# The attention blocks in another order: the four first blocks of the batches at the start

## The chip, the cores and the metric

The kernel runs on one core of a Trainium2 chip. The metric is device time in microseconds (us) of one execution, as the median of several runs. PE is TensorE, DVE is VectorE, ACT is ScalarE, POOL is GpSimd, and SP is the queue that issues nearly all transfers.

## What is computed

Attention with a local window of 96 keys and 8 global keys, with a linear distance bias per head, and behind it a feed-forward layer. Shapes: 4 batches, 8 heads, 768 positions, head width 64; the layer goes from 512 to 2048 and back, over 3072 tokens.

```
scores = scale * np.matmul(q, k.transpose(0, 1, 3, 2))
...
keep = is_global | is_local
...
bias = -slopes[:, None, None] * dist[None, :, :]
scores = scores + bias[None, :, :, :]
scores = np.where(keep, scores, -1000000000.0)
scores = scores - np.max(scores, axis=-1, keepdims=True)
a = np.exp(scores)
a = a / (np.sum(a, axis=-1, keepdims=True) + 1e-09)
return np.matmul(a, v).astype(np.float32)
...
h = x @ w_in
g = h * (1.0 / (1.0 + np.exp(-1.702 * h)))
return (g @ w_out).astype(np.float32)
```

## The kernel before

**Blocks.** A block is 128 positions of one batch, all 8 heads. There are 24, numbered n in the order in which they are worked; before, that is batch by batch, so that blocks 0, 6, 12 and 18 are the first of a batch. A first block sees 128 keys (its own). Every other block sees 256: its own 128, and 128 that stand for the block before it with the 32 leading keys of the batch written over its first 32 (which hold the global ones).

**Two forms.** Blocks 0 to 3 (n < EARLY) go through `first`. It computes the scores once with queries in rows (matmuls into the tile `s`, the mask `mm` added by one more matmul with a unit matrix, a DVE reduction into `top` for the largest), turns the largest with `aux` and `mT`, and computes the scores again with keys in rows (`sT`: product, mask, and the largest subtracted by a third matmul). ACT takes the exponential into `pt`, and f32 matmuls of `pt` with `VF` give `pv`; a 65th column of ones gives the sum. Blocks 0 and 1 (n < FIRST) do the products in f32 from `QZ` and `KF`, turned by PE; blocks 2 and 3 do them as pairs of f16 halves from `QK`, turned by a DMA transpose.

Blocks 4 to 23 go through `unit`, four units of two heads each: scores `s`, a DVE pass that adds the mask and takes the largest (`p`, `NM`), the exponential on ACT, a split in f16 halves `hl` (a cast on ACT, a subtraction on DVE), a DMA transpose into `pt`, and three 64-column matmuls into `pv` for every head and 128 keys.

**What a block needs of the one before.** `leading` writes the 32 leading keys and values of the batch, kept in `KG` and `VG`, over the first rows of a block that is done, so that the next block can use it. `handover` fills the places where this isn't there yet: for block 2 it builds keys (`QKover2`, by a load, a split, a DMA transpose and two copies) and values, for block 4 values.

**The layer.** Two blocks make a chunk c of 256 tokens (c = 0 to 11). `finish` makes `xT` of a block. Chunks 0 to 2 run `up` (tile `h`, from the up weights `w`) and `down` (tile `y`) for 8 slices s of the layer, in plain form. Chunks 3 to 11 run `up_two`, with fewer products over sums of weights (`T`, made by `twist`) and of inputs (`xS`), tiles `pa` and `pb`. The 16 weight tiles (up and down of 8 slices) are loaded as 64-bit words and converted: two passes on ACT, two on DVE, a cast on ACT, and a subtraction on DVE that ends a tile (`w`).

**What sets the order.** All of this is written as tasks with a cost for each engine and a due time. `Work.order` runs through time, gives each engine the ready task that is due first, and writes every engine's instructions in that order; each engine then works its queue in that order. In the first 50 us of that plan PE gets filler matmuls (`idle`) where it has nothing else. The due times of the layer follow T0, PACE0 and SKEW: SKEW is how many slices chunk 1 runs behind chunk 0.

PSUM is eight banks, used by rings: `r_s` and `r_pv` with one buffer each, `r_h` with two, and four `r_y`. Before, the scores of blocks 0 and 1 alternate between `r_s` and `r_y[1,1]`. `r_QK` has three buffers and `r_raw` two.

## Time and profile before

| | us |
|---|---|
| median of 3 runs | 622.38 (621.77 to 622.87) |
| the profiled execution, time | 621.17 |
| the profiled execution, span | 619.4 |
| PE busy | 599.5 (97%) |
| PE weight load busy | 453.0 (73%) |
| DVE busy | 503.8 (81%) |
| ACT busy | 480.1 (78%) |
| POOL busy | 3.9 (1%) |

The span is from the first instruction of the profiled execution to its last; the execution's own time is 1.8 us longer. Matmuls are pipelined and their ends are modelled: what one costs PE in a full stretch is the distance between the starts of two, not its own duration. DVE and ACT are busy for four fifths of the span, but not evenly.

### The profile page before, as it was taken

How to read it: one execution, taken by the hardware profiler on the slowest of the kernel's cores; microseconds unless marked ns; L12 is line 12 of the kernel's file. 1: busy time of each engine (PE TensorE's matmuls, PEld its weight loads, DVE VectorE, ACT ScalarE, POOL GpSimd, SP SyncE). 2: the span in 40 equal slices, each digit the busy share in tenths (PEclk: the TensorE clock that was granted, in tenths of full speed). 3: DMA queues.
4: the chain of work that ended last, by engine and by line, in shares of the span. 5: the costliest groups of instructions: out<-in, count | busy, mean ns of one | idle time of the engine just before them, and what ended most of it. 6: DMA issues, size and time to landing. Idle time of an engine off the chain costs nothing.

```text
span 619.4 us, 17131 instructions
## 1 busy us (share of the span) xinstructions
PE 599.5 (97%) x6871; PEld 453.0 (73%) x6874; DVE 503.8 (81%) x1175; ACT 480.1 (78%) x1100; POOL 3.9 (1%) x16
## 2 busy tenths in 40 slices
PE   7989998999999999999999999999999999999995
PEld 4867876776777776777777777776767767777895
DVE  5778899999999969869979989888878978856441
ACT  3778999967967978779978988987988977924432
POOL 2000000000000000000000000000000000000000
PEclk9999999999999999999999999999999999999998
DMA  8999887999777668799999999999999999510001
GB/s 190 246 265 302 252 283 156 186 187 175 161 155 141 123 147 158 140 177 204 173 204 205 217 206 190 202 234 195 192 229 211 207 199 216 135 35 3 35 3 39
DMA packets 260854, 108.01 MB, mean 174 GB/s; under 512 B 241664, under 2 KB 242176, under 8 KB 260768
## 3 DMA queue, kind: packets, MB, share of 16 engines
q1 hardware_dynamic: 260480, 106.85, 84.4%
q8 instruction: 55, 0.90, 0.6%
q14 instruction: 31, 0.25, 0.1%
q10 hardware_dynamic: 288, 0.00, 0.0%
HBM read 56.43 MB, written 6.29 MB: 101 GB/s over the span
## 4 chain that ended last, share of the span: by engine, by line
PE 72%; DVE 11%; DMA 8%; ACT 5%; issue 3%; SPq 0%; POOL 0%; DVEq 0%; ACTq 0%; POOLq 0%
PE y L905 31%; PE pa L839 12%; PE pb L839 9%; PE h L799 8%; PE s L526 4%; DMA pt<-hl 4%; DMA QK<-qk 1%; PE pv L557 1%; DVE w L367 1%; PE pv L559 1%; PE pv L558 1%; PE pv L633 1%; ACT p L542 1%; DMA raw<-in_k_dram 1%; DVE hl L547 1%
## 5 line engine op out<-in xcount | busy, mean ns | idle before, releaser
L905 PE MATMUL y<-w,g 128*128 128x512 f16 (+1 forms) x1248 | 268.4, 363 | 0.3 <-DVE g L811 0.2
L905 PEld LDWEIGHTS <-g 128*128 128x128 f16 x1248 | 117.6, 98 | 102.1 <-DVE g L811 1.1
L839 PEld LDWEIGHTS <-w 128*128 128x128 f16 x1728 | 101.4, 98 | 6.0
L542 ACT ACTIVATE p<-p,NM 128x256 f32<-128x256 f32 (+1 forms) x160 | 77.2, 485 | 4.5 <-DVE NM L532 4.3
L839 PEld LDWEIGHTS <-T 128*128 128x128 f16 x1296 | 76.6, 98 | 4.5 <-issue 0.2
L799 PE MATMUL h<-xT,w 128*128 128x256 f16 x576 | 69.7, 273 | 2.3 <-DVE xT L705 1.4
L547 DVE TENSOR_TENSOR hl<-p,hl 128x512 f16<-128x512 f32 (+1 forms) x80 | 51.7, 646 | 15.5 <-ACT hl L546 15.1
L799 PEld LDWEIGHTS <-w 128*128 128x128 f16 x576 | 55.4, 98 | 12.0 <-issue 2.6
L532 DVE CUSTOM_DVE_ANT_0 p<-s,mm 128x256 f32<-128x256 f32 (+1 forms) x160 | 58.2, 398 | 6.0 <-PE s L526 5.8
L871 ACT ACTIVATE t<-h 128x512 f32<-128x512 f32 (+1 forms) x72 | 36.2, 518 | 25.3 <-DVE h L847 25.0
L880 DVE SCALAR_TENSOR_TENSOR g<-t,g 128x512 f16<-128x512 f32 x72 | 49.0, 687 | 7.8 <-ACT g L879 7.2
L847 DVE TENSOR_TENSOR h<-pb,h 128x256 f32<-128x256 f32 x72 | 29.1, 419 | 28.5 <-PE pb L839 26.5
L546 ACT CAST hl<-p 128x512 f16<-128x512 f32 (+1 forms) x80 | 46.9, 586 | 6.5 <-DMA pt<-hl 4.5
L879 ACT ACTIVATE g<-t 128x512 f16<-128x512 f32 x72 | 44.8, 628 | 7.5 <-DVE t L872 7.5
L839 PE MATMUL pa<-xS,T 128*128 128x128 f16 x648 | 45.0, 219 | 0.0
L526 PEld LDWEIGHTS <-QK 128*128 128x128 f16 x592 | 36.9, 98 | 7.2 <-DVE NM L532 3.1
L872 DVE SCALAR_TENSOR_TENSOR t<-t,h 128x512 f32<-128x512 f32 (+1 forms) x72 | 38.3, 552 | 4.7 <-ACT t L871 4.0
L526 PE MATMUL s<-QK 128*128 128x128 f16 x320 | 38.5, 219 | 0.0
L839 PE MATMUL pb<-xS,w 128*128 128x128 f16 x540 | 37.5, 219 | 0.0
L839 PE MATMUL pa<-xT,w 128*128 128x128 f16 x540 | 37.2, 219 | 0.0
L526 PE MATMUL s<-QK,QK 128*128 128x128 f16 x272 | 33.9, 219 | 2.0 <-DVE NM L532 2.0
L557 PE MATMUL pv<-VR,pt 128*128 128x64 f16 x288 | 33.9, 193 | 1.8 <-DMA pt<-hl 1.5
(193 smaller groups left out, 1103.0 us busy)
## 6 DMA issues: line engine op xcount, KB each, us to landing
ws<-in_moe_w_in_dram SPq DMA_DIRECT2D x8, 1024.0 KB, 7.2
ws<-in_moe_w_out_dram SPq DMA_DIRECT2D x8, 1024.0 KB, 8.0
raw<-in_q_dram SPq DMA_DIRECT2D x24, 256.0 KB, 3.9
raw<-in_k_dram SPq DMA_DIRECT2D x24, 256.0 KB, 4.9
QK<-QK SPq DMA_DIRECT2D x44, 128.0 KB, 3.7
out_dram<-yo SPq DMA_DIRECT2D x22, 256.0 KB, 2.9
raw<-in_v_dram SPq DMA_DIRECT2D x20, 256.0 KB, 4.3
ws_00again<-in_moe_w_in_dram SPq DMA_DIRECT2D x8, 512.0 KB, 4.8
```

The costliest lines, as they stand in the source:

```text
L526: nc.tensor.matmul(sp()[:, j, s * P:(s + 1) * P], d["QK"]()[:, 0, h, :], K[:, 1 + z, h, :], start=(z == 0), stop=(z == 1), skip_group_chec ...
L532: nc.vector.tensor_tensor_reduce(out=pr()[:, j, :], in0=sp()[:, j, :], in1=m, scale=-1.0 / SC, scalar=3.0e38, op0=ALU.add, op1=ALU.min, ac ...
L542: ex.append(add({"ACT": 0.28 + 0.105 * ns}, lambda e, j=j: nc.scalar.activation(pr()[:, j, :], pr()[:, j, :], AF.Exp, bias=NM[:, n, hs[j]: ...
L546: t4 = add({"ACT": 0.1 + 0.215 * ns}, lambda e: nc.scalar.copy(hl()[:, 0], pr()), ex, [pr, hl])
L547: t5 = add({"DVE": 0.07 + 0.265 * ns}, lambda e: nc.vector.tensor_sub(hl()[:, 1], pr(), hl()[:, 0]), [t4], [pr, hl])
L557: nc.tensor.matmul(o, ph, V[:, 0, h], start=(s == 0), stop=False, skip_group_check=True)
L799: nc.tensor.matmul(ph()[:, fi, :], w1(s, cc, z, fi), X[:, y, cc, :], start=(j + cc == 0), stop=(j == 2 and cc == NCC - 1))
L839: nc.tensor.matmul(o()[:, fi], w, x()[:, y * NCC + 2 * k + cc, t], start=(first and fi + j + cc == 0), stop=(last and j + cc == 3), skip_g ...
L872: return add({"DVE": 0.08 + 0.265 * w}, lambda e: nc.vector.scalar_tensor_tensor(o(), o(), 1.0, src(), ALU.add, ALU.mult), [t1], srcs)
L879: t4 = add({"ACT": 0.53}, lambda e, g=g, tt=tt: nc.scalar.mul(g()[:, 0], tt(), SG / (SX * SW)), u, [tt, g])
L880: t5 = add({"DVE": 0.61}, lambda e, g=g, tt=tt: nc.vector.scalar_tensor_tensor(g()[:, 1], tt(), SG / (SX * SW), g()[:, 0], ALU.mult, ALU.s ...
L905: nc.tensor.matmul(y(), part(zg, f), w2(s, z, f % 2)[:, m], start=(begin and f + j == 0), stop=(end and j == 2 and f == 2 * len(steps) - 1 ...
```

## The change

The blocks get another numbering. `place(n)` gives batch and position: n = 0 to 3 are the first blocks of the four batches, and n = 4 to 23 are the positions 1 to 5 of batch 0, of batch 1, and so on. All four blocks of `first` now see 128 keys, and its code has one key block left: two passes of four heads each, where there were four of two. All 20 blocks of `unit` see 256 keys. Where a batch goes on (n = 4, 9, 14, 19), `handover` loads the k and v of its first block once more and builds `QKover`, `VRover`, `KG` and `VG` from them. The scores of all four first blocks go through `r_s`. Chunk rows of the output follow `place`. T0, PACE0 and SKEW are lower.

```diff
+    def place(n):
+
+        return (n, 0) if n < EARLY else ((n - EARLY) // (NB - 1), 1 + (n - EARLY) % (NB - 1))
+
     def load(n, raw, parts=(0, 1, 2)):
-        b, i = divmod(n, NB)
+        b, i = place(n)
...
-    def handover(n, keys, whole):
-
-        b = n // NB
-        d = prev[n] = dict(blk[n - 1], VG=[])
+    def handover(n):
+
+        b = place(n)[0]
+        d = prev[n] = {}
         raw = Buf(r_raw, [P, 3, H, D], F32, f"over{n}")
-        if keys:
-            d["G"] = []
-            d["QK"] = Buf(r_QK, [P, 3, H, P], F16, f"QKover{n}")
-            d["qk_ready"] = turn_halves(f"over{n}", raw, d["QK"], rows_before(n, k, lambda: raw()[:, 1], raw), 1)
-            keep_keys(b, d)
...
+        d["QK"] = Buf(r_QK, [P, 3, H, P], F16, f"QKover{n}")
+        d["VR"] = Buf(r_VR, [P, 2, H, D], F16, f"VRover{n}")
+        ld = load(b, raw, (1, 2))
+        d["qk_ready"] = turn_halves(f"over{n}", raw, d["QK"], ld[:1], 1)
+        d["v_ready"] = d["VG"] = halves(d["VR"], raw, ld[1:])
+        d["G"] = []
+        keep_keys(b, d)
+        keep_values(b, d)
...
     def unit(n, u, want_s, want_v):
 
-        b, i = divmod(n, NB)
-        ns = 1 if i == 0 else 2
+        ns = 2
...
     def first(n, want):
 
-        b, i = divmod(n, NB)
-        ns = 1 if i == 0 else 2
-        W = ns * P
         d = blk[n]
...
-        spare = r_y[1, 0] if n < 2 else r_y[1, 1]
         mT = mTs[n % 2]
-        aux = d["aux"] = Buf(spare, [P, 2 * P], F32, f"aux{n}")
+        aux = d["aux"] = Buf(r_y[1, n % 2], [P, 2 * P], F32, f"aux{n}")
...
-        for u in range(NU):
-            sp = Buf(r_y[1, 1] if n < 2 and u % 2 else r_s, [P, 2, W], F32, f"s{n}_{u}")
+        for f in range(2):
+            sp = Buf(r_s, [P, 4, P], F32, f"s{n}_{f}")
...
-                for j in range(2):
-                    h = 2 * u + j
-                    for s in range(ns):
-                        for z, (qp, kp) in enumerate(products(h, s)):
-                            nc.tensor.matmul(sp()[:, j, s * P:(s + 1) * P], qp, kp, start=(z == 0), stop=False,
-                                             skip_group_check=True)
-                    m = mm[:, h, 2] if ns == 1 else mm[:, h, 0:2].rearrange("p a c -> p (a c)")
-                    nc.tensor.matmul(sp()[:, j, :], id16, m, start=False, stop=True, skip_group_check=True)
+                for j in range(4):
+                    h = 4 * f + j
+                    for z, (qp, kp) in enumerate(products(h)):
+                        nc.tensor.matmul(sp()[:, j], qp, kp, start=(z == 0), stop=False, skip_group_check=True)
+                    nc.tensor.matmul(sp()[:, j], id16, mm[:, h, 2], start=False, stop=True, skip_group_check=True)
...
-        for u in range(NU):
-            sT = Buf(r_y[0, u % 2] if n < 2 else r_y[1, 0], [P, 2 * ns, P], F32, f"sT{n}_{u}")
-            pt = Buf(r_pt, [P, 2 * ns, P], F32, f"pt{n}_{u}")
+        for f in range(2):
+            sT = Buf(r_y[0, f], [P, 4, P], F32, f"sT{n}_{f}")
+            pt = Buf(r_pt, [P, 4, P], F32, f"pt{n}_{f}")
...
-                    for s in range(ns):
-                        nc.tensor.matmul(o, pt()[:, j * ns + s, :], both[ns - 1 - s]["VF"]()[:, h],
-                                         start=(s == 0), stop=(s == ns - 1), skip_group_check=True)
...
+                    nc.tensor.matmul(o, pt()[:, j, :], d["VF"]()[:, h], start=True, stop=True, skip_group_check=True)
...
     def leading(n):
 
-        b, i = divmod(n, NB)
+        b, i = place(n)
         d = blk[n]
         d["G"], d["VG"] = [], []
-        if i == NB - 1 or i == 0 or n == FIRST - 1:
+        if i == NB - 1 or n < EARLY:
             return
...
+        b, i = place(2 * c + t)
+        row = (b * NB + i) * P
...
-                    out[(2 * c + t) * P:(2 * c + t + 1) * P, m], yo()[:, m]), [t2], [yo], want + 6)
+                    out[row:row + P, m], yo()[:, m]), [t2], [yo], want + 6)
...
-    T0, PACE0, PACE, PACE2, LAG, SKEW, LEAD = 25.0, 7.0, 5.9, 5.7, 16.0, 6, 68.0
+    T0, PACE0, PACE, PACE2, LAG, SKEW, LEAD = 20.0, 6.0, 5.9, 5.7, 16.0, 3, 68.0
...
-        if n in (FIRST, EARLY):
+        if n >= EARLY and place(n)[1] == 1:
             wk.tag = f"over{n}"
-            handover(n, n == FIRST, n < EARLY)
+            handover(n)
```

`rows_before` is gone. What comes of it in the engines' queues, at three places:

DVE, from the end of the mask of the other keys to the end of the first weight tile; `top` is the reduction of the scores, `s0_2` is the third part of block 0. Before:

```order
L325 SCALAR_TENSOR_TENSOR mk_165<-flt_146,nnl_90 128x32
L608 TENSOR_REDUCE top_84<-s0_0_213 128x2
L608 TENSOR_REDUCE top_84<-s0_1_218 128x2
L333 TENSOR_SCALAR mm_89<-mk_165 128x256 x8
L608 TENSOR_REDUCE top_84<-s0_2_231 128x2
L608 TENSOR_REDUCE top_84<-s0_3_244 128x2
L361 TENSOR_SCALAR wa0_0_267<-ws0_0_152 128x1024
L365 ISA wa0_0_267<-wa0_0_267,w0_0_249 128x2048
L608 TENSOR_REDUCE top_84<-s1_0_257 128x2
L608 TENSOR_REDUCE top_84<-s1_1_274 128x2
L448 SCALAR_TENSOR_TENSOR qk162_0_282<-raw2_185,qk162_0_282 128x16x64
L367 SCALAR_TENSOR_TENSOR w0_0_249<-wa0_0_267,w0_0_249 128x1024
L608 TENSOR_REDUCE top_84<-s1_2_304 128x2
```

After:

```order
L326 SCALAR_TENSOR_TENSOR mk_167<-flt_148,nnl_90 128x32
L583 TENSOR_REDUCE top_84<-s0_0_215 128x4
L334 TENSOR_SCALAR mm_89<-mk_167 128x256 x8
L583 TENSOR_REDUCE top_84<-s0_1_230 128x4
L362 TENSOR_SCALAR wa0_0_264<-ws0_0_154 128x1024
L366 ISA wa0_0_264<-wa0_0_264,w0_0_247 128x2048
L583 TENSOR_REDUCE top_84<-s1_0_255 128x4
L446 SCALAR_TENSOR_TENSOR qk162_0_270<-raw2_187,qk162_0_270 128x16x64
L368 SCALAR_TENSOR_TENSOR w0_0_247<-wa0_0_264,w0_0_247 128x1024
L583 TENSOR_REDUCE top_84<-s1_1_284 128x4
L587 CAST mT1_80<-aux1_325 8x128
L362 TENSOR_SCALAR wa0_1_354<-ws0_1_275 128x1024
```

Eight reductions of blocks 0 and 1 have become four, each over four heads.

ACT, where chunk 1 begins: `t1_0` is the tanh of slice 0 of chunk 1, `w7_0` and `w4_0` are up weights of slices 7 and 4 of chunk 0. Before:

```order
L364 ACTIVATE w7_0_1234<-ws7_0_1138 128x1024
L808 ACTIVATE t0_6_1251<-h0_6_1200 128x512
L457 ACTIVATE VR4_1260<-raw4_871 128x512
L396 ACTIVATE junk_88,s2_85<-raw4_871 128x512
L366 ACTIVATE w6_1_1191<-wa6_1_1236 128x1024
L810 ACTIVATE g0_6_1267<-t0_6_1251 128x512
L457 ACTIVATE VRover4_1271<-over4_1049 128x512
L366 ACTIVATE w7_0_1234<-wa7_0_1248 128x1024
L363 ACTIVATE w7_1_1288<-ws7_1_1154 128x1024
L364 ACTIVATE w7_1_1288<-ws7_1_1154 128x1024
L808 ACTIVATE t1_0_1321<-h1_0_1275 128x512
```

After:

```order
L365 ACTIVATE w4_0_813<-ws4_0_717 128x1024
L771 ACTIVATE t0_3_837<-h0_3_795 128x512
L367 ACTIVATE w3_1_765<-wa3_1_761 128x1024
L445 ACTIVATE qk16over4_1_849<-over4_752 128x8x64
L367 ACTIVATE w4_0_813<-wa4_0_827 128x1024
L773 ACTIVATE g0_3_863<-t0_3_837 128x512
L364 ACTIVATE w4_1_867<-ws4_1_809 128x1024
L365 ACTIVATE w4_1_867<-ws4_1_809 128x1024
L367 ACTIVATE w4_1_867<-wa4_1_885 128x1024
L771 ACTIVATE t1_0_923<-h1_0_888 128x512
```

Slice 0 of chunk 1 stood behind the weights of slice 7, and now stands behind those of slice 4.

SP, around the end of block 8's units (`pt8_3` is the last); block 9 is the fourth of batch 1 before, and the first after the first of batch 1 now. Before:

```order
L450 DMA_TRANSPOSE QK9_2373<-qk169_0_2159 128x16x128
L548 DMA_TRANSPOSE pt7_2_2406<-hl7_2_2346 128x8x128
L548 DMA_TRANSPOSE pt7_3_2423<-hl7_3_2395 128x8x128
L452 DMA QK9_2373<-QK9_2373 64x1024 x2
L548 DMA_TRANSPOSE pt8_0_2528<-hl8_0_2490 128x8x128
L660 DMA VR7_2032<-VG1_1880 32x1024
L382 DMA raw10_2349<-in_v_dram 128x8x64
L712 DMA_TRANSPOSE xT3_2302<-x167_2560 128x8x128
L382 DMA raw11_2628<-in_q_dram 128x8x64
L548 DMA_TRANSPOSE pt8_1_2630<-hl8_1_2573 128x8x128
```

After:

```order
L535 DMA_TRANSPOSE pt8_1_2422<-hl8_1_2395 128x8x128
L675 DMA_TRANSPOSE xT3_2232<-x167_2453 128x8x128
L387 DMA raw11_2498<-in_q_dram 128x8x64
L448 DMA_TRANSPOSE QKover9_2512<-qk16over9_1_2229 128x8x128
L468 DMA VG1_2529<-VRover9_2424 32x1024
L387 DMA raw11_2498<-in_k_dram 128x8x64
L535 DMA_TRANSPOSE pt8_2_2559<-hl8_2_2471 128x8x128
L387 DMA raw11_2498<-in_v_dram 128x8x64
L450 DMA QKover9_2512<-QKover9_2512 64x1024 x2
L535 DMA_TRANSPOSE pt8_3_2602<-hl8_3_2563 128x8x128
```

Block 9's own keys were the last it needed; now a second transpose and two copies, `QKover9`, stand between blocks 8 and 9.

## Rows read from the trace of the kernel before

**Rows 1.** Busy us of each engine by stretch: length, PE, PEld, DVE, ACT, POOL, PEclk, DMA.

```profile
0.00:45.00 45.00, 37.81 (x284) 29.11 (x288) 30.81 (x80) 27.73 (x35) 3.89 (x16) 1.00 1.02 229
45.00:75.00 30.00, 29.82 (x297) 24.12 (x295) 24.40 (x36) 26.90 (x32) 0.00 (x0) 1.00 1.00 291
75.00:110.00 35.00, 31.88 (x288) 24.21 (x286) 33.82 (x54) 32.67 (x48) 0.00 (x0) 1.00 0.86 216
110.00:200.00 90.00, 89.01 (x851) 63.72 (x849) 86.22 (x187) 71.75 (x169) 0.00 (x0) 1.00 0.90 167
200.00:500.00 300.00, 298.05 (x3771) 221.78 (x3768) 258.34 (x645) 258.85 (x670) 0.00 (x0) 1.00 0.99 190
```

**Rows 2.** PE in order of time: start, us, instruction, count, idle before and its releaser.

```profile
13.49 0.49 PE L601 MATMUL s<-KF,QZ 128*128 128x128 f32 x2 [0.29 <-DVE top L608]
...
43.65 2.34 PE L799 MATMUL h<-xT,w 128*128 128x256 f16 x20 [1.36 <-DVE xT L705]
```

**Rows 3.** The same view: steps of the two forms, for the distance of starts.

```profile
11.61 0.44 PE L601 MATMUL s<-KF,QZ 128*128 128x128 f32 x2
11.94 0.44 PE L601 MATMUL s<-KF,QZ 128*128 128x128 f32 x2
...
17.16 0.61 PE L601 MATMUL s<-KF,QZ 128*128 128x128 f32 x4
17.71 0.61 PE L601 MATMUL s<-KF,QZ 128*128 128x128 f32 x4
...
18.61 0.44 PE L624 MATMUL sT<-QZ,KF 128*128 128x128 f32 x2
18.99 0.44 PE L624 MATMUL sT<-QZ,KF 128*128 128x128 f32 x2
...
34.87 3.29 PE L633 MATMUL pv<-VF,pt 128*128 128x65 f32 x28
37.99 0.61 PE L633 MATMUL aux<-VF,pt 128*128 128x65 f32 x4
...
75.11 0.28 PE L601 MATMUL s<-QK,QK 128*128 128x128 f16 x2
75.44 0.28 PE L601 MATMUL s<-QK,QK 128*128 128x128 f16 x2
...
83.30 0.27 PE L624 MATMUL sT<-QK,QK 128*128 128x128 f16 x2
83.52 0.28 PE L624 MATMUL sT<-QK 128*128 128x128 f16 x2
...
114.05 0.19 PE L557 MATMUL pv<-VRover,pt 128*128 128x64 f16 x1
114.08 0.19 PE L558 MATMUL pv<-VRover,pt 128*128 128x64 f16 x1
```

**Rows 4.** DVE groups by shape: count, busy us, mean ns of one, idle before.

```profile
L532 DVE CUSTOM_DVE_ANT_0 p<-s,mm 128x256 f32<-128x256 f32 x136 | 52.2, 418 | 5.3 <-PE s L526 5.1
L547 DVE TENSOR_TENSOR hl<-p,hl 128x512 f16<-128x512 f32 x68 | 46.7, 687 | 13.5 <-ACT hl L546 13.1
L608 DVE TENSOR_REDUCE top<-s 128x2 f32<-128x512 f32 x12 | 8.1, 685 | 3.1 <-PE s L604 3.1
L532 DVE CUSTOM_DVE_ANT_0 p<-s,mm 128x128 f32<-128x128 f32 x24 | 6.0, 285 | 0.6 <-PE s L526 0.6
L547 DVE TENSOR_TENSOR hl<-p,hl 128x256 f16<-128x256 f32 x12 | 5.0, 419 | 2.0 <-ACT hl L546 2.0
```

**Rows 5.** In order of time: the up weights of slice 4 are done; chunk 3 starts.

```profile
72.91 1.22 DVE L367 SCALAR_TENSOR_TENSOR w<-wa,w 128x1024 f16<-128x1024 f32 x1
...
204.84 0.83 PE L839 MATMUL pa<-xT,w 128*128 128x128 f16 x12
```

**Rows 6.** Transfers: count, KB each, median us from issue to landing.

```profile
QK<-QK SPq DMA_DIRECT2D x44, 128.0 KB, 3.7
...
QKover<-qk16over SPq DMA_TRANSPOSE x1, 5.7
```

More of the change, by code (lines that the diff above doesn't have):

```diff
@@ L523, in scores @@
                 for s in range(ns):
-                    K = d["QK"]() if s == ns - 1 else before["QK"]()
+                    K = (before, d)[s]["QK"]()
                     for z in range(2):
@@ L539, in unit @@
         for j in range(2):
-            t2 = add({"DVE": 0.09 + 0.15 * ns}, lambda e, j=j: rows(e, j), [t1, M1 if ns == 1 else M2], [sp, pr])
+            t2 = add({"DVE": 0.09 + 0.15 * ns}, lambda e, j=j: rows(e, j), [t1, M2], [sp, pr])
             checks.append(t2)
@@ L554, in values @@
                 for s in range(ns):
[L555 removed]
+                    V = (before, d)[s]["VR"]()
                     ph, pl = pt()[:, j * ns + s, :], pt()[:, (2 + j) * ns + s, :]
@@ L562, in unit @@
             d["pv"] = Buf(r_pv, [P, H, D], F32, f"pv{n}")
-        t7 = add({"PE": 6 * ns * MM64}, values, [t6, *d["v_ready"], *(before["VG"] if ns == 2 else [])],
-                 [pt, d["pv"], d["VR"]] + ([before["VR"]] if ns == 2 else []), want_v)
+        t7 = add({"PE": 6 * ns * MM64}, values, [t6, *d["v_ready"], *before["v_ready"], *before["VG"]],
+                 [pt, d["pv"], d["VR"], before["VR"]], want_v)
         d.setdefault("V", []).append(t7)
@@ L568, in first @@
     def first(n, want):
-        b, i = divmod(n, NB)
-        ns = 1 if i == 0 else 2
-        W = ns * P
         d = blk[n]
-        before = prev.get(n, blk.get(n - 1)) if ns == 2 else None
-        both = [d, before][:ns]
-        spare = r_y[1, 0] if n < 2 else r_y[1, 1]
         mT = mTs[n % 2]
-        aux = d["aux"] = Buf(spare, [P, 2 * P], F32, f"aux{n}")
+        aux = d["aux"] = Buf(r_y[1, n % 2], [P, 2 * P], F32, f"aux{n}")
         pv = d["pv"] = Buf(r_pv, [P, H - 1, D + 1], F32, f"pv{n}")
-        QKs = [x_[f] for x_ in both for f in (("QZ", "KF") if n < FIRST else ("QK",))]
@@ L581, in first, with products @@
-        VFs = [x_["VF"] for x_ in both]
-        def products(h, s):
-            o = both[ns - 1 - s]
+        QKs = [d[f] for f in (("QZ", "KF") if n < FIRST else ("QK",))]
+        def products(h):
             if n < FIRST:
-                return [(d["QZ"]()[:, h // 2, h % 2, :], o["KF"]()[:, h // 2, :])]
-            return [(d["QK"]()[:, 0, h, :], o["QK"]()[:, 1 + z, h, :]) for z in range(2)]
+                return [(d["QZ"]()[:, h // 2, h % 2, :], d["KF"]()[:, h // 2, :])]
+            return [(d["QK"]()[:, 0, h, :], d["QK"]()[:, 1 + z, h, :]) for z in range(2)]
@@ L631, in values @@
                     o = pv()[:, h] if h < H - 1 else aux()[:, P:P + D + 1]
-                    for s in range(ns):
-                        nc.tensor.matmul(o, pt()[:, j * ns + s, :], both[ns - 1 - s]["VF"]()[:, h],
-                                         start=(s == 0), stop=(s == ns - 1), skip_group_check=True)
-            t4 = add({"PE": 2 * ns * (mm_s + 2 * MM128)}, turned, [t3, *there], [sT, *QKs], want + 6.0 + 1.2 * u)
+                    nc.tensor.matmul(o, pt()[:, j, :], d["VF"]()[:, h], start=True, stop=True, skip_group_check=True)
@@ L637, in first @@
+            t4 = add({"PE": 4 * (mm_s + 2 * MM128)}, turned, [t3, M1, *d["qk_ready"]], [sT, *QKs], want + 6.0 + 1.2 * f)
             d["S"].append(t4)
             blk.setdefault(("mT", n), []).append(t4)
-            t5 = add({"ACT": 0.06 + 0.22 * ns}, lambda e, sT=sT, pt=pt: nc.scalar.activation(pt(), sT(), AF.Exp, scale=1.0 / SC),
-                     [t4], [sT, pt])
-            t6 = add({"PE": 2 * ns * FP65}, values, [t5, *d["v_ready"], *((before["v_ready"] + before["VG"]) if ns == 2 else [])],
-                     [pt, pv, aux, *VFs], want + 8.0 + 1.2 * u)
+            t5 = add({"ACT": 0.5}, lambda e, sT=sT, pt=pt: nc.scalar.activation(pt(), sT(), AF.Exp, scale=1.0 / SC), [t4], [sT, pt])
@@ L643, in first @@
+            t6 = add({"PE": 4 * FP65}, values, [t5, *d["v_ready"]], [pt, pv, aux, d["VF"]], want + 8.0 + 1.2 * f)
             d.setdefault("V", []).append(t6)
     def leading(n):
-        b, i = divmod(n, NB)
+        b, i = place(n)
         d = blk[n]
         d["G"], d["VG"] = [], []
-        if i == NB - 1 or i == 0 or n == FIRST - 1:
+        if i == NB - 1 or n < EARLY:
             return
-        KG = blk["KG", b]
+        KG, VG = blk["KG", b], blk["VG", b]
         d["G"].append(add({"DVE": 0.22}, lambda e: nc.vector.tensor_copy(
```

78 lines of the change are left out of this document (26 added, 52 removed).

## The prediction

> **What bounds the kernel now.** I read the stretches first: busy time of each engine by stretch [rows 1]. PE is short of full by 7.2 us in the first 45 us, by 3.3 from 45 to 110 and by 1.0 from 110 to 200; from 200 to 500 it is idle for 2.0 of 300 us. So from about 45 us on it is PE's own work that sets the time, and a us of it saved there is a us, unless another engine is next. The same rows name the next one: DVE is busy for 33.8 + 86.2 = 120.0 of the 125 us from 75 to 200, and for 258.3 of 300 us (86%) after that. Before 75 us it has 75 - 55.2 = 19.8 us idle. The granted clock is 1.00 in all of these stretches, the one with the 7.2 us of waits too, so I put no price on the clock. Then I read PE in order of time: the layer's first matmuls run until 43.65, and there the second half of chunk 0 has to wait for block 1's xT [rows 2]; chunk 3 starts at 204.84 [rows 5]. The two marks cut the run into a start, a front (both limits near) and a rest (PE alone).
>
> **PE's work, removed.** Prices are distances between starts [rows 3]. Block 1, in f32: a head's scores take 17.71 - 17.16 = 0.55 us with 256 keys and 11.94 - 11.61 = 0.33 with 128, so 8 heads save 1.8; the turned scores take 18.99 - 18.61 = 0.38 for a head and 128 keys, 8 of them 3.0; the values of seven heads and 256 keys take 37.99 - 34.87 = 3.12 for 14 matmuls (28 instructions, two passes each), 0.22 each, 8 of them 1.8. That is 6.6 us. Blocks 2 and 3, in halves of f16: scores 75.44 - 75.11 = 0.33 a head, of which half goes, 1.3 for 8; turned 83.52 - 83.30 = 0.22, 1.8 for 8; values again 1.8. That is 4.9 us a block, 9.8 for two. Sum: 16.4 us, all of it ahead of chunk 3.
>
> **PE's work, added.** Blocks 6, 12 and 18 go through the units with 256 keys. Each gets 16 matmuls of 128 columns at 0.22 / 4 = 0.055 and 24 of 64 columns at 114.08 - 114.05 = 0.03 [rows 3]: 0.9 + 0.7 = 1.6 us, 4.8 for three, of which 3.2 (blocks 12 and 18) fall behind chunk 3's start. Net on PE: -11.6 us. The four lists of matmuls for the layer itself are the same in number.
>
> **DVE.** The reductions of the first blocks were 12 over 512 columns at 0.685 and four half as wide (at no less than half of that, some 1.5 together), 9.7 us; they become 8 at 0.685, 5.5 us: -4.2. Blocks 6, 12 and 18 pay 8 x (0.418 - 0.285) + 4 x (0.687 - 0.419) = 2.1 us more each, +6.4 [rows 4]. A handover splits 128x512 keys and 128x512 values; there was one split of each and there will be four, six more at the price of the nearest row of that shape, 0.687 [rows 4]: +4.1. Over the whole run DVE gets +6.3 us on 504, 84% of the new time. It stays behind PE as a mean. Before chunk 3, though, only block 6 and the handovers of blocks 4 and 9 count: -4.2 + 2.1 + 1.4 = -0.7. **DVE saves nearly nothing in the stretch where it is full.**
>
> **The start.** Block 1 is 6.6 us shorter on PE before the first layer matmul, and its x with it. Against that stands one thing. The scores of blocks 0 and 1 now all use one bank, so that each part waits for the reduction of the part before it. The row shows what that costs where it happened already: 0.29 us of idle behind a filler, with a reduction of 0.685 inside [rows 2, 4]; about 1.0 us a time (estimate). There were two such places and there are three, the first of block 1 included. So I expect the layer to start 6 to 9 us sooner than 43.65. Blocks 2 and 3 have layer matmuls between their two parts in the new order, which cover the reduction.
>
> The Trainium skill (Perfetto Trace Analysis, Matmuls) speaks against this edit: independent matmul groups should rotate through different PSUM banks, so that the evacuation of one overlaps the matmuls of the next. By that rule all seven changes of a part would be paid and the sum would come out some 4 us higher, at 618; by the row in group 2 only the two or three without other work between them are.
>
> **The front.** Two limits set when chunk 3 starts. PE alone: -16.4 + 1.6 = -14.8 us. DVE alone: its full stretch begins with the layer and the weights, so it moves with the start by 6 to 9, and by the 0.7: -7 to -10. What lets it do better is that some of its work before 204.84 isn't due there (the T sums of the later slices, the splits of blocks 10 and 11) and can slide to where it has 14% free. What holds it back is the weights: in the new order slice 4 of chunk 0 stands on PE ahead of chunk 1, its weights were done at 72.91 + 1.22 [rows 5], and PE, with 10 us less of blocks 2 and 3 to fill the time, will be there early. I take -12.5, a little nearer to PE's end than to the middle of the two limits, because SKEW 3 gives PE a second chunk to work on from slice 4 on, where it had none until slice 7.
>
> **The rest.** +3.2 us for blocks 12 and 18. At a handover (blocks 9, 14 and 19) a new chain stands between two blocks: a buffer of QK comes free with the last scores of the block before, then the transpose, 5.7 us to landing, then two copies, 3.7 [rows 6], then the first scores. That is 9.4 us and what SP has ahead of it. Counted in the new order with the prices above, PE has 9.8, 14.5 and 11.9 us of other work there. Behind the waiting transpose on SP stand loads and the pt transposes of the same block, which its values need. Bounds: 0 if all three are covered, 6 if each lacks 2 us; I take 0.8, since only the first is short. The loads of k and v themselves (0.5 MB each time) are issued long before and cost nothing as long as SP isn't behind. The output rows and the lower T0 and PACE0 have no price of their own.
>
> **Sum.** -12.5 + 3.2 + 0.8 = -8.5 us against the profiled execution's 621.2, which is 612.7. The median of the runs is 1.2 us above that execution, so 613.9.
>
> **Rivals.** (1) **PE is the only bound** all the way: for it speaks that PE waited for DVE little even where DVE was full (1.0 us of 90 idle); against it, that 96% leaves DVE no room for a faster PE. Front -14.8, up to 2 more if the start's waits shrink, then +3.2 and 0: 609 to 611. (2) **The weights or DVE keep their time**: chunk 0's later slices come when they came, and PE waits between 45 and 110 us instead of working on blocks 2 and 3. The front gains 3 to 6 instead of 12.5; with +4.0 behind it, 620 to 623. For it speaks 24.4 + 26.9 of 30 us on DVE and ACT from 45 to 75 [rows 1], which is when the weights are converted; against it the earlier start. (3) **The handover is the new wait**: queues are in order, so a late QKover holds PE's scores and everything behind them. From (8.5 + 0.8) / 3 = 3.1 us a time the gain is gone; at 5 us a time, which a transpose stuck behind full DMA engines could give (0.99 busy from 200 to 500 [rows 1]), 15 us stand in place of 0.8: 628, slower than before.
>
> **How the numbers follow.** Forecast 0.46 (609 to 618), rival 1 0.28, rival 2 0.15 (two thirds of it still faster), rival 3 0.11. What a measurement of this kernel can tell from no change is about 0.2%, 1.2 us: faster 0.46 + 0.28 + 0.10 = 0.84, same 0.05, slower 0.11. The range reaches from 605 (rival 1 with a start better than I think) to 621.5 (into rival 2), and leaves out rival 3 and a part of rival 2, under 0.2.
>
> **What will show it.** The first layer matmul waiting for block 1's xT at 34 to 38 us instead of 43.65. Chunk 3's pa at about 192 instead of 204.84; at 190 or less rival 1, at 198 or more rival 2. PE idle from 45 to 110 us: up to 8 us in the forecast, over 12 in rival 2. DVE 95% or more from 70 us to chunk 3. PE's longest waits for QKover at blocks 9, 14 and 19 under 2 us each; rival 3 shows them at 5. From chunk 3 to the end 4 us more than the 414.6 of before. I am wrong in kind if the front is shorter and the rest longer by as much, and wrong in size if DVE's idle before 75 us doesn't shrink.

## The result and the profile after

The changed kernel takes 615.48 us in the median (614.86 to 616.96), the kernel before 622.08 beside it: a ratio of 0.990, with a 95% interval of 0.987 to 0.993. That is 6.6 us less; the prediction said 8.5 less. The profiled execution took 614.86 us, with a span of 613.0.

Busy time by stretch, as in [rows 1], for the changed kernel (length, PE, PEld, DVE, ACT, POOL, PEclk, DMA share, GB/s):

```profile
0.00:45.00 45.00, 37.51 (x289) 28.42 (x290) 31.63 (x79) 27.60 (x32) 3.89 (x16) 0.96 0.99 241
45.00:75.00 30.00, 26.85 (x232) 20.60 (x231) 26.93 (x40) 26.20 (x34) 0.00 (x0) 1.00 1.06 257
75.00:110.00 35.00, 34.21 (x299) 23.91 (x297) 32.56 (x59) 34.91 (x60) 0.00 (x0) 1.00 1.18 266
110.00:200.00 90.00, 87.33 (x874) 63.18 (x873) 87.87 (x185) 74.42 (x166) 0.00 (x0) 1.00 0.89 178
200.00:500.00 300.00, 295.89 (x3803) 221.84 (x3801) 260.35 (x641) 262.76 (x671) 0.00 (x0) 1.00 1.01 197
```

From 45 to 75 us PE now waits for 3.15 us where it waited for 0.2, and DVE works 2.5 us more; from 75 to 110 it is the other way round for PE. DVE is at 97.6% from 110 to 200.

PE in order of time, the answer to [rows 2] and to the second row of [rows 5] (start, length, instruction, idle before and its releaser):

```profile
32.60 0.63 PE L664 MATMUL tx<-ident,x 128*128 128x128 f32 x4 [1.24 <-DVE x L644]
34.37 1.01 PE L1028 MATMUL idle<-idle 128*128 128x512 bf16 x2 [1.14 <-DVE xT L668]
36.45 3.42 PE L762 MATMUL h<-xT,w 128*128 128x256 f16 x24
...
42.14 0.27 PE L586 MATMUL aux<-ident,top 128*8 128x128 f32 x1 [1.17 <-DVE top L583]
...
53.92 0.27 PE L586 MATMUL aux<-ident,top 128*8 128x128 f32 x1 [1.07 <-DVE top L583]
55.38 0.22 PE L599 MATMUL sT<-mT,id 128*128 128x128 bf16 x1 [1.02 <-ACT mT L587]
...
193.91 0.50 PE L802 MATMUL pa<-xT,w 128*128 128x128 f16 x6
```

The row at 36.45 holds all 24 `h` matmuls of chunk 0's first slice: the four of the first half, which started at 41.68 before, and the 20 of the second half, which started at 43.65. Taken one by one, the fifth of them starts at 37.31, so the second half is 6.3 us sooner (the `xT` that it waited for is done at 36.66 instead of 43.59, 6.9 sooner; the slow clock, below, takes the rest). Chunk 3 starts at 193.91 instead of 204.84 (10.9 sooner). The waits are of another kind than before: at 42, 54 and 55 us PE stands in the chain of blocks 2 and 3 from the reduction (`top`) by way of `aux` and `mT` to `sT`.

The two stretches ahead of chunk 3's start and from it on; first the kernel before, then the changed one:

```profile
0.00:204.84 204.84, 193.35 (x1751) 144.35 (x1755) 179.96 (x364) 162.29 (x285) 3.89 (x16) 1.00 0.93 206
204.84:619.40 414.56, 406.17 (x5123) 308.68 (x5120) 323.88 (x812) 317.82 (x816) 0.00 (x0) 1.00 0.81 159
```

```profile
0.00:193.91 193.91, 179.81 (x1590) 130.74 (x1591) 173.04 (x344) 157.55 (x275) 3.89 (x16) 0.99 1.01 224
193.91:613.00 419.09, 409.94 (x5211) 312.54 (x5208) 334.51 (x827) 327.48 (x826) 0.00 (x0) 1.00 0.83 165
```

This is the account of these two executions. In the front PE works 13.54 us less and waits 2.6 us more (14.10 against 11.49); behind it PE works 3.77 us more and waits 0.76 more. DVE has 6.9 us less in the front and 10.6 more behind it.

The front's clock is 0.99 because it fell for a moment, which it did nowhere in the front of the kernel before. The changed kernel, 34 to 40 us:

```profile
34.00:36.00 2.00, 1.63 (x10) 1.07 (x10) 2.00 (x4) 2.00 (x4) 0.00 (x0) 0.58 1.15 367
36.00:38.00 2.00, 2.00 (x16) 1.58 (x14) 2.00 (x4) 1.22 (x2) 0.00 (x0) 0.56 1.61 103
38.00:40.00 2.00, 2.00 (x24) 1.82 (x22) 1.86 (x3) 2.00 (x2) 0.00 (x0) 1.00 1.01 224
```

So PE ran mostly at the lower of its two levels (1.2 GHz) here, right behind the waits of 1.24 and 1.14 us: 0.42 x 1.63 + 0.44 x 2.00 = 1.6 us of the 179.81 are work that took longer. Without it the front's work has fallen by 15.1 us, against 14.8 in the prediction.

Where the clock falls isn't set by the instructions alone. The variant with more PE work in blocks 13 to 18 (below) has the same instructions in the same order up to chunk 3, and the same waits of 1.24 and 1.14 us. In its profiled execution the clock is 1.00 from 34 to 38, and falls from 42 to 48 and from 56 to 62 us:

```profile
42.00:44.00 2.00, 1.71 (x22) 1.58 (x23) 1.86 (x4) 1.22 (x2) 0.00 (x0) 0.84 1.03 383
44.00:46.00 2.00, 2.00 (x18) 1.80 (x16) 2.00 (x4) 1.94 (x4) 0.00 (x0) 0.50 1.04 309
58.00:60.00 2.00, 2.00 (x22) 2.00 (x20) 2.00 (x3) 1.34 (x2) 0.00 (x0) 0.50 1.00 372
```

There the same sum gives some 3.1 us instead of 1.6, and chunk 3 starts at 196.32 instead of 193.91. So a start of chunk 3 that is read from one trace can be off by 2 to 3 us, and where a variant's gain or loss falls, ahead of chunk 3 or behind it, is no more certain than that.

DVE's groups, the answer to [rows 4] (count, busy, mean ns, idle before):

```profile
L519 DVE CUSTOM_DVE_ANT_0 p<-s,mm 128x256 f32<-128x256 f32 x160 | 61.4, 420 | 7.4 <-PE s L513 6.5
L534 DVE TENSOR_TENSOR hl<-p,hl 128x512 f16<-128x512 f32 x80 | 55.0, 688 | 9.4 <-ACT hl L533 9.0
...
L583 DVE TENSOR_REDUCE top<-s 128x4 f32<-128x512 f32 x8 | 5.5, 689 | 0.2 <-PE s L579 0.2
```

The two passes of the units rose from 52.2 + 6.0 and 46.7 + 5.0 by 6.5 us together (predicted 6.4); the eight reductions cost what was said. And the handover, the answer to [rows 6] (count, KB, us to landing):

```profile
QKover<-QKover SPq DMA_DIRECT2D x8, 128.0 KB, 3.5
...
QKover<-qk16over SPq DMA_TRANSPOSE x4, 4.5
```

The chain is 8.0 us instead of the 9.4 assumed. No PE wait for `QKover` is in the trace. PE's costliest waits in the changed kernel (total, times, longest):

```profile
PE aux L586 <- DVE top L583: 2.2, 2, 1.2
PE y L870 <- DVE g L774: 2.0, 2, 1.3
PE pb L802 <- ACT h L807: 1.7, 2, 1.3
PE s L578 <- DVE top L583: 1.4, 2, 1.0
```

### The profile page after: what moved, and what is told of

Read it like the earlier page. It is cut to its first block, busy times and chain, and to the rows that moved or that the text cites. A ratio compares the mean times of both kernels' runs of the same rounds, so it can differ in the third digit from the quotient of the medians.

```text
span 613.0 us, 17039 instructions
## 1 busy us (share of the span) xinstructions
PE 589.7 (96%) x6798; PEld 443.3 (72%) x6798; DVE 507.5 (83%) x1170; ACT 485.0 (79%) x1101; POOL 3.9 (1%) x16
## 4 chain that ended last, share of the span: by engine, by line
PE 50%; DVE 19%; DMA 12%; ACT 10%; issue 6%; SPq 1%; DVEq 0%; POOL 0%; ACTq 0%; POOLq 0%
PE y L870 22%; PE pa L802 10%; PE pb L802 7%; DMA QK<-qk 3%; DMA pt<-hl 3%; PE s L513 3%; DVE p L519 2%; ACT p L529 2%; PE h L762 2%; DVE hl L534 2%; DMA QK<-QK 2%; DVE t L772 1%; DMA ws_01again<-in_moe_w_in_dram 1%; DVE t L708 1%; ACT junk L394 1%
## 5 line engine op out<-in xcount | busy, mean ns | idle before, releaser
L529 ACT ACTIVATE p<-p,NM 128x256 f32<-128x256 f32 x160 | 79.7, 501 | 6.9 <-DVE NM L519 6.7
L519 DVE CUSTOM_DVE_ANT_0 p<-s,mm 128x256 f32<-128x256 f32 x160 | 61.4, 420 | 7.4 <-PE s L513 6.5
L762 PEld LDWEIGHTS <-w 128*128 128x128 f16 x576 | 55.6, 99 | 10.9 <-DVE w L368 0.7
L534 DVE TENSOR_TENSOR hl<-p,hl 128x512 f16<-128x512 f32 x80 | 55.0, 688 | 9.4 <-ACT hl L533 9.0
L533 ACT CAST hl<-p 128x512 f16<-128x512 f32 x80 | 49.3, 616 | 2.5 <-DMA pt<-hl 0.6
L513 PEld LDWEIGHTS <-QK 128*128 128x128 f16 x640 | 39.2, 98 | 6.4 <-DVE NM L519 2.5
L513 PE MATMUL s<-QK 128*128 128x128 f16 x320 | 40.0, 219 | 0.8 <-DMA QK<-QK 0.8
L544 PE MATMUL pv<-VR,pt 128*128 128x64 f16 x288 | 35.0, 193 | 1.1 <-DMA pt<-hl 1.1
L545 PE MATMUL pv<-VR,pt 128*128 128x64 f16 x288 | 35.0, 193 | 0.0
```

What stands on the lines that cost most here:

```text
L513: nc.tensor.matmul(sp()[:, j, s * P:(s + 1) * P], d["QK"]()[:, 0, h, :], K[:, 1 + z, h, :], start=(z == 0), stop=(z == 1), skip_group_chec ...
L519: nc.vector.tensor_tensor_reduce(out=pr()[:, j, :], in0=sp()[:, j, :], in1=m, scale=-1.0 / SC, scalar=3.0e38, op0=ALU.add, op1=ALU.min, ac ...
L529: ex.append(add({"ACT": 0.28 + 0.105 * ns}, lambda e, j=j: nc.scalar.activation(pr()[:, j, :], pr()[:, j, :], AF.Exp, bias=NM[:, n, hs[j]: ...
L533: t4 = add({"ACT": 0.1 + 0.215 * ns}, lambda e: nc.scalar.copy(hl()[:, 0], pr()), ex, [pr, hl])
L534: t5 = add({"DVE": 0.07 + 0.265 * ns}, lambda e: nc.vector.tensor_sub(hl()[:, 1], pr(), hl()[:, 0]), [t4], [pr, hl])
L762: nc.tensor.matmul(ph()[:, fi, :], w1(s, cc, z, fi), X[:, y, cc, :], start=(j + cc == 0), stop=(j == 2 and cc == NCC - 1))
```

## The experiments

Each was measured beside the kernel before, whose median was between 620.8 and 621.9 in these comparisons; ratios are to it, with 95% intervals. Two of these ratios can be told apart from some 0.4% on, about 2 us. The changed kernel has 0.990 [0.987, 0.993].

### Is it the retiming (T0, PACE0, SKEW) or the blocks?

The retiming alone, in the kernel before:

```
-    T0, PACE0, PACE, PACE2, LAG, SKEW, LEAD = 25.0, 7.0, 5.9, 5.7, 16.0, 6, 68.0
+    T0, PACE0, PACE, PACE2, LAG, SKEW, LEAD = 20.0, 6.0, 5.9, 5.7, 16.0, 3, 68.0
```

> The kernel before with nothing changed but T0, PACE0 and SKEW (20, 6, 3). Theory A: chunk 1 cannot start sooner, since blocks 2 and 3 with 256 keys are late; 621 to 624, no change. Rival B: 616 to 618, most of the gain.

Measured: 622.76 us, 1.003 [1.001, 1.005]; chunk 3 at 205.19. By itself it brings nothing.

The changed kernel with the old constants (the same two lines the other way round):

> The changed kernel with the T0, PACE0 and SKEW of before (25, 7, 6). Theory A, the work that left PE is what counts: chunk 1 comes later into the order, but the time stays within 2 us of the changed kernel's 615.5 (so 5 to 8 us under before). Rival B, the new due times bring the gain: 620 or more, and chunk 3 starts at 200 us or later instead of 193.9.

Measured: 620.47 us, 0.999 [0.997, 1.000]; chunk 3 at 196.90. Nearly the whole gain is gone; by the traces 3.0 us of that stand ahead of chunk 3's start and 3.5 behind it (422.6 us instead of 419.1), and why behind it stays open. Ahead of it PE stands before the later weights (4.7 us from 40 to 110 us, where the changed kernel has 0.5) and the clock falls behind it:

```profile
75.00:80.00 5.00, 2.02 (x13) 0.94 (x11) 4.90 (x11) 4.99 (x7) 0.00 (x0) 1.00 0.94 303
80.00:85.00 5.00, 3.73 (x17) 2.48 (x18) 5.00 (x8) 4.02 (x5) 0.00 (x0) 0.54 0.94 307
```

Of the three constants, SKEW alone at 6:

> The changed kernel with SKEW back at 6 (chunk 1 joins chunk 0's slices six steps later instead of three), T0 and PACE0 as in the changed kernel. With all three constants back the time was 620.47, and PE stood waiting between 73 and 89 us, the granted clock at 0.54 from 80 to 85. If it is the second chunk that covers PE while the later weights are made, this one falls back as well, to 619 to 621, with 8 us or more of PE idle between 45 and 110 us. If the earlier start and pace are what counts, it stays within 1.5 us of 615.5.

Measured: 624.88 us (622.01 to 628.42), 1.006 [1.003, 1.009]; chunk 3 at 202.0 in the profiled execution, which took 622.43. The changed kernel with SKEW 6, by stretch:

```profile
45.00:75.00 30.00, 27.74 (x214) 21.59 (x212) 25.26 (x34) 27.71 (x35) 0.00 (x0) 0.89 0.94 272
75.00:110.00 35.00, 27.98 (x232) 19.20 (x232) 31.94 (x59) 31.80 (x53) 0.00 (x0) 1.00 1.04 221
```

PE is idle for 9.3 us from 45 to 110 instead of 3.9, and the clock falls between 45 and 75. Of the 9.3 us, 2.5 are waits for weights. SKEW is a constant that counts: the shorter blocks take away work with which PE used to fill the time in which DVE and ACT make the later weights, and chunk 1, three steps behind chunk 0, takes its place. What T0 and PACE0 add beside SKEW 3 wasn't measured. That this one is slower than the one before it, with T0 and PACE0 back as well, isn't explained by SKEW; the plan differs in much else.

One step further, SKEW 2:

> The changed kernel with SKEW 2 instead of 3: chunk 1 joins chunk 0's slices one step sooner. SKEW 6 cost 9 us against 3, with PE idle for 9.3 us between 45 and 110. If chunk 1 is what covers PE while the weights are made, 2 covers as well or better: 613 to 616. If chunk 1 then needs its blocks 2 and 3 before they are done, PE waits for their x between 45 and 60 us and the time is 617 or more.

Measured: 618.28 us, 0.996 [0.994, 0.998]. The time is that of the second expectation, the waits are not quite: PE waits 3.6 us for the reductions between the two halves of the scores of blocks 2 and 3 (1.7 at 37 and 1.9 at 51 us), which the layer's matmuls no longer cover, but the `xT` that it waits for (2.3 us) is block 1's, at 33 us, ahead of the layer. None is the x of blocks 2 and 3.

### Is it the start of the layer, or its clock?

The changed kernel with a second PSUM bank for the second half of the scores of blocks 0 and 1 (the order is planned anew):

```
-            sp = Buf(r_s, [P, 4, P], F32, f"s{n}_{f}")
+            sp = Buf(r_h if n < FIRST and f else r_s, [P, 4, P], F32, f"s{n}_{f}")
```

> The changed kernel with the second half of the scores of blocks 0 and 1 in r_h instead of r_s, so that a half need not wait for the reduction of the one before. If the waits of one bank set the start: the first layer matmul at 35.5 us or sooner instead of 36.45, and 0.5 to 1.5 us off the time. If something behind the start is late anyway (the wait of PE from 52 to 57 us on DVE and ACT): the start moves and the time stays within 0.5 us.

Measured: 615.56 us, 0.991 [0.988, 0.994]. The layer's first matmul comes 5.3 us sooner (31.12 instead of 36.45) and the second half of chunk 0 4.6 us sooner (32.70 instead of 37.31); chunk 3 starts at 193.78 instead of 193.91. The clock falls here too, from 54 to 60 us, and costs 1.6 us by the same sum, so it doesn't hide a gain. Nothing of a sooner start arrives.

The changed kernel with five filler matmuls behind block 1's values and five behind its transposes, where PE waits at 32 and 34 us:

```
+                if n == 1 and f == 1:
+                    for _ in range(5):
+                        nc.tensor.matmul(sT(), idle[:, 0:P], idle, start=True, stop=True)
...
+                for _ in range(5 if n == 1 else 0):
+                    nc.tensor.matmul(d["bank"](), idle[:, 0:P], idle, start=True, stop=True)
```

> The changed kernel, same order, with five filler matmuls behind block 1's last values and five behind its transposes, where PE waited 1.24 and 1.14 us and the granted clock fell to 0.58 and 0.56 from 34 to 38 us. If the clock's fall costs what the rows show (s and h of chunk 0: 1.2 us longer than at full clock): clock 1.00 from 34 to 38 us, h from 35.4 to 38 us. In the time: minus 1.2 us if PE sets the stretch that follows, within 0.4 us if PE then waits for DVE, ACT or weights from 52 us on anyway (theory A of two limits).

Measured: 615.61 us, 0.991 [0.989, 0.994]. The clock stayed at 1.00 from 34 to 38 and fell behind PE's later waits, from 42 to 48 and from 56 to 62 us. This variant:

```profile
34.00:38.00 4.00, 3.47 (x32) 2.40 (x31) 4.00 (x6) 3.23 (x5) 0.00 (x0) 1.00 1.15 231
40.00:42.00 2.00, 0.14 (x1) 0.00 (x0) 2.00 (x4) 1.81 (x3) 0.00 (x0) 1.00 1.03 227
42.00:44.00 2.00, 1.69 (x25) 1.56 (x26) 1.86 (x4) 1.21 (x2) 0.00 (x0) 0.95 0.98 365
44.00:46.00 2.00, 2.00 (x16) 1.69 (x15) 2.00 (x4) 1.93 (x4) 0.00 (x0) 0.50 1.05 323
```

The wait for block 2's reduction is 1.99 us here (1.17 in the changed kernel, and it ends at the same time in both, 42.13 and 42.14: there the slow matmuls ahead of it had used up a part). But that the fillers moved the fall isn't shown: the variant with more PE work in blocks 13 to 18 has no fillers, and the same falls at the same places. The falls cost some 3.3 us here, more than in the changed kernel's trace, and chunk 3 starts at 197.4; the time is the same. So this run doesn't tell what a front without any fall would bring. The single executions tell a little: of the twelve of the changed kernel and of the two variants of this section, the three with a mean granted clock of 0.998 or more took 614.08, 614.48 and 615.10 us (all three are of the variants), the nine others 614.86 to 617.00, on average 615.96. That is some 1.4 us, by few executions.

### What limits the front: PE, or DVE as well?

More PE, nothing else: the turned products of blocks 2 and 3 (with mask and largest, four matmuls a head) four times over.

```
+                    for _ in range(4 if n >= FIRST else 1):
+                        for z, (qp, kp) in enumerate(products(h)):
...
```

> The changed kernel in the same order, in which the turned products of blocks 2 and 3 (16 heads of 128 keys) are issued four times over into the same bank, so that PE has about 10.7 us more (48 more products at 0.22) in the front and no other engine has more. If PE is the only bound there, the time rises by all of it, 10 to 11 us. If DVE and the weights limit the front as well, part of it fills waits: PE's idle time from 45 to 110 us (3.9 us in the changed kernel) and its later short waits go first, and the time rises by 4 to 8 us.

Measured: 631.72 us, 1.016 [1.013, 1.020], 16.2 us more than the changed kernel for 10.7 us of work (at least 12.4 by the ends of the two intervals). Both expectations were too low. This variant, busy time from 45 to 75, and DVE in order of time there:

```profile
45.00:75.00 30.00, 27.90 (x351) 25.04 (x349) 17.58 (x30) 16.51 (x22) 0.00 (x0) 0.97 0.76 203
```

```profile
44.53 2.36 DVE L368 SCALAR_TENSOR_TENSOR w<-wa,w 128x1024 f16<-128x1024 f32 x2
52.68 0.69 DVE L775 SCALAR_TENSOR_TENSOR g<-t,g 128x512 f16<-128x512 f32 x1 [5.79 <-ACT g L774]
```

DVE stands for 5.79 us, because what is next in its queue needs a `g` that comes out of PE's layer matmuls behind the longer block. In the stretch it works 9.4 us less than in the changed kernel (17.58 against 26.93), the last step of the last weight tile starts at 134.4 instead of 122.4, and chunk 3 starts at 207.1, 13.2 us later. In the front PE has 10.5 us more of work and 2.8 more of waits, and DVE 12.2 more of idle time. So PE's work between the layer's slices costs its own length, and DVE, which is full later on, stands meanwhile; that this is what makes it dearer than its length is argued, since 2.8 us is no more than two traces of the same front differ by. Another 4.3 us are behind chunk 3's start, where nothing was changed; PE waits 4.3 us in this run for transposed `pt`, instead of 1.1. That is one trace; why it should be so stays open.

More DVE, nothing else: one more copy of 128x512 behind each of the 16 weight tiles.

```
-        t5 = add({"DVE": 1.15}, lambda e: nc.vector.tensor_add(ai(), ai(), extra()), [t2, t3, t4], [w, wa])
+        t5 = add({"DVE": 1.15}, lambda e: (nc.vector.tensor_add(ai(), ai(), extra()), nc.vector.tensor_copy(w()[:, 1, 0:512], wa()[:, 0:512])),
+                 [t2, t3, t4], [w, wa])
```

> The changed kernel in the same order on every engine, with one more copy of 128x512 on DVE behind the last addition of each of the 16 weight tiles. Nothing reads more than before, but each tile is finished some 0.69 us later, 11 us of DVE in all, between about 35 and 122 us. If DVE and the weights limit the front (they were busy for 87.87 of 90 us from 110 to 200 in the changed kernel), chunk 3 starts 5 to 11 us later than 193.91 and the time rises by 3 to 9 us, part of it given back behind 200 us, where DVE has 13% free. If PE alone sets the time from 45 us on, the time rises by 0 to 2 us.

Measured: 619.94 us, 0.997 [0.995, 0.999], 4.5 us more than the changed kernel; chunk 3 at 198.8. The copy was cheaper than written: its row in this variant is

```profile
L366 DVE CAST w<-wa 128x512 f16<-128x512 f32 x16 | 6.8, 427 | 0.7
```

that is 6.8 us, not 11. Some two thirds of it arrive in the time. By these two traces all of it is in the front (193.91 to 198.8, 4.9); against 196.32, the other start of chunk 3 with this order, it would be 2.5. PE alone, for which 0 to 2 were expected, isn't what sets the front. (The copy stands ahead of each tile's last steps, so it makes the weights later as well as DVE's work longer; the run doesn't part the two.)

Less DVE: the eight sums of weight halves given to POOL.

```
-        t1 = add({"DVE": 2.3}, lambda e: [nc.vector.tensor_add(f(), w()[:, 0], w()[:, 1]) for f, w in zip(fs, ws_)],
+        t1 = add({"POOL": 4.6}, lambda e: [nc.gpsimd.tensor_add(f(), w()[:, 0], w()[:, 1]) for f, w in zip(fs, ws_)],
```

> The changed kernel with the eight sums of two halves of a weight slice (128x1024, 1.222 us each on DVE between 124.8 and 195.5, 9.8 us in all) given to POOL, which does nothing after the start; the order is planned anew with 4.6 us for two of them. It takes 9.8 us off DVE where DVE was busy for 87.87 of 90 us. Eleven us more on DVE in the front cost 4.4 us. If DVE's load there is a limit, the time falls by 2 to 4 us, to 611.5 to 613.5, and chunk 3 starts before 192. If the load is not what holds the front, or if DVE's own instructions become longer while POOL works, it stays within 1.5 us of 615.5 or rises.

Measured: 615.1 us, 0.991 [0.989, 0.992], the same as the changed kernel. DVE's busy time from 110 to 200 didn't fall either (87.75 against 87.87). Its groups in that stretch, first the changed kernel, then this one:

```profile
L534 DVE TENSOR_TENSOR hl<-p,hl 128x512 f16<-128x512 f32 x16 | 11.0, 687 | 0.3 <-ACT hl L533 0.3
L774 DVE SCALAR_TENSOR_TENSOR g<-t,g 128x512 f16<-128x512 f32 x15 | 10.3, 687 | 0.0
L732 DVE TENSOR_TENSOR T<-t,T 128x1024 f16<-128x1024 f32 x6 | 7.2, 1221 | 0.0
```

```profile
L534 DVE TENSOR_TENSOR hl<-p,hl 128x512 f16<-128x512 f32 x16 | 14.8, 926 | 0.1
L774 DVE SCALAR_TENSOR_TENSOR g<-t,g 128x512 f16<-128x512 f32 x15 | 12.7, 845 | 0.0
L732 DVE TENSOR_TENSOR T<-t,T 128x1024 f16<-128x1024 f32 x6 | 8.6, 1440 | 0.0
```

The same groups became longer by 3.8 + 2.4 + 1.4 = 7.6 us, most of the 9.8 that were moved. The means hide that it is a few single instructions, those that met one of POOL's (last section). What the second half of the expectation named came true; whether DVE's load can be lowered with profit this run doesn't tell, since it wasn't lowered. (This variant's profiled execution took 619.43 us, 4.3 above its median; it is used for the instructions' lengths alone.)

### The rest: what are PE's work and the handovers worth there?

The changed kernel with blocks 6, 12 and 18 on their own keys:

```
-        ns = 2
+        ns = 1 if n in (6, 12, 18) else 2
...
-                    K = (before, d)[s]["QK"]()
+                    K = (before, d)[s + 2 - ns]["QK"]()
...
```

> The changed kernel in which the units of blocks 6, 12 and 18 (the kernel before's batch starts) take their own keys only, 128 instead of 256, as they did in the kernel before; their scores and values for the other keys and the wait for those are left out. The order is planned anew. It takes back the 1.6 us a block of PE and 2.1 us a block of DVE that the prediction put on the change: 4.8 us of PE, 3.2 of them behind chunk 3. If the term is right and a us of PE in the rest is a us of time, the time falls by 3 to 5 us against the changed kernel, most of it behind chunk 3's start. If other engines hold PE there, it falls by less than 2 us.

Measured: 612.44 us, 0.985 [0.981, 0.989], 3.0 us less. PE's busy time falls by 5.3 us (589.7 to 584.4; predicted 4.8). By the trace the time falls not where it was expected: chunk 3 starts 2.3 us sooner, and from there on it takes 419.9 us against 419.1. But 2.3 us is what two traces of the same front differ by, and this trace's execution is 0.9 us above its median, the changed kernel's 0.6 below, so where the 3.0 us fall stays open. PE's gaps have opened behind chunk 3's start (12.6 us instead of 9.2); the row of 400 to 450 us, in which it was busy for 49.36 in the changed kernel:

```profile
400.00:450.00 50.00, 46.48 (x579) 34.07 (x577) 38.98 (x99) 41.86 (x110) 0.00 (x0) 1.00 1.06 205
```

The opposite, in the same order: the scores of blocks 13 to 18 twice.

```
-                for s in range(ns):
+                for s in (0, 0, 1, 1) if 13 <= n <= 18 else range(ns):
```

> The changed kernel in the same order, in which the score matmuls of blocks 13 to 18 are issued twice into the same place: 192 more matmuls of 128 columns at 0.0557, 10.7 us of PE, far behind the front, where PE is busy for 295.89 of 300 us; no other engine has more to do. If PE alone sets the time there, the time rises by 10 to 11 us. If DVE and ACT (87% busy each) share in it, part of it takes the place of waits and the time rises by 5 to 9 us. Against the same 10.7 us in blocks 2 and 3, which cost 16.2, it also tells whether a us of PE is worth more at the start than later.

Measured: 623.72 us, 1.004 [1.002, 1.006], 8.2 us more for 10.7 of work: the second expectation. From 200 to 500 PE is now busy for

```profile
200.00:500.00 300.00, 298.08 (x3919) 227.73 (x3918) 256.46 (x632) 257.62 (x655) 0.00 (x0) 1.00 0.96 191
```

298.08 of 300 us against 295.89: 2 us of waits were filled. A us of PE is worth about 0.8 here, and 1.5 among blocks 2 and 3.

Without the handovers of blocks 9, 14 and 19:

```
+        if n > EARLY:
+            d = prev[n] = dict(blk[n - 1], G=[], VG=[])
+            keep_keys(b, d)
+            keep_values(b, d)
+            return
```

> The changed kernel without the handovers of blocks 9, 14 and 19: their units take the keys and values of the block before them (of the batch before) for the other 128 keys, so that the second load, the split of keys and values, the transpose and the two copies are left out three times; block 4 keeps its handover. The order is planned anew. By the prediction's price (0.8 us of waiting for PE at the three places, and six splits of 0.687 on DVE that are hidden) the time falls by 0 to 2 us against the changed kernel. If the handover chain holds PE (rival 3 in a small form), or if DVE's 4 us and the SP queue count in the rest, it falls by 3 us or more.

Measured: 616.11 us, 0.993 [0.991, 0.996], 0.6 us more than with them by the medians, 0.3% by the ratios, within what two of these can tell. Three handovers cost nothing that can be measured.

No variant that computes the same is faster than the changed kernel by more than the measurement can tell.

## Why the prediction was right, and where its size was off

**Sum.** The direction, the mechanism and the range held: 615.48 against 613.9, in 605 to 621.5. The forecast's case, 609 to 618, is the one that came.

**PE's work** was priced well: 15.1 us less in the front at an even clock, 14.8 said; 3.77 more behind it, 3.2 said.

**The front** is the term that was mis-sized: -10.9 in the profiled execution, not -12.5 (and -8.5 by the other trace with this front). Its step "PE alone: -14.8" came true as work, and 1.6 us went to the clock and 2.6 to more waiting. "I put no price on the clock", drawn from rows that showed 1.00 all along, failed: PE's waits in the first 45 us are about as long as before in sum (7.5 against 7.2 us) and singly (at most 1.3 against 1.4), but they fall elsewhere, and the clock fell at 34 us in this kernel's trace, at 42 and 56 in the other with the same front. "The new order covers the reduction" of blocks 2 and 3 held between their two halves, but not for the step behind, `top` to `aux` to `mT`, with 1.17, 1.07 and 1.02 us of wait.

**DVE.** "Saves nearly nothing in the stretch where it is full" was right by what is due there, and the way out that the prediction named did the rest: DVE's work in the front fell by 6.9 us and rose by 10.6 behind it, so work slid to where it had room. In all it rose by 3.7 us, not 6.3: the units (+6.5), the reductions (-4.1) and the splits (+4.1) came as said, but the planner gave 2.2 us of casts and output copies to ACT, which it may choose. Its share from 70 us to chunk 3 was 95.4%, as forecast.

**The start** came 6.3 us sooner for the second half of chunk 0, inside 6 to 9. But the second bank moved it by another 4.6 us, and chunk 3 and the time stayed where they were. So the prediction's step that DVE's limit "moves with the start" is not borne out. What sets the front is not when the layer starts but PE and DVE together from there on: more DVE cost two thirds of itself, more PE one and a half times itself.

**SKEW.** The prediction gave SKEW 3 as a reason to lean to PE's end. It was more than that: without it the gain is gone (624.88), and alone it is worth nothing (622.76, with T0 and PACE0). In the sum it weighed 0.8 us, from -11.7, the middle of the two limits (-14.8 and -7 to -10), to -12.5; by the runs 5.0 us (with T0 and PACE0) to 9.4 us hang on it, and the blocks with the old constants bring 0.1%. So a us of PE's work saved in the front was a us only because SKEW 3 came with it. The forecast was for both together, so its total doesn't show how far off this share was.

**Rival 1** (PE alone) is out by the front: chunk 3 at 193.91 (196.32 in the other trace), above 190, and 0.65 us of time for each us of DVE. **Rival 2** didn't come either: PE waits 3.9 us from 45 to 110, where over 12 were its mark. The weights did become later (the last step of the last one starts at 122.4 instead of 108.8), and PE waited for weights for 0.5 us only; that this is because with two chunks under way fewer matmuls stand right behind them is argued. With SKEW 6 it comes near to rival 2: chunk 3 at 202.0, above its 198, and 9.3 us of waits from 45 to 110, below its 12. **Rival 3** is out: no wait for `QKover`, and nothing gained by taking three handovers away.

**The rest** took 4.5 us more instead of 4.0: 3.77 of work and 0.76 of waits. The waits were not the handovers', and the 0.8 that I put on these should have been 0. "PE alone" is too strong for this part: PE's work there weighs about 0.8 a us where it was added, and where it was taken out, the waits grew in its place by that trace.

**The rule on PSUM banks.** The Trainium skill (Perfetto Trace Analysis, Matmuls) would have had independent groups rotate through banks. At the one place where this was tried the start came sooner by 4.6 us, as the rule says, and the time didn't move, since the start isn't the limit. With SKEW 2, where less stands between the halves of blocks 2 and 3, PE did wait 3.6 us in the one bank, and the time was 2.8 us longer; what a second bank would do there wasn't tried.
